# Expert 1's tokens gathered as whole rows and turned on TensorE, in a routed mixture of experts on one core

## The chip, the cores and the metric

The kernel runs on one core of one Trainium2 chip. The metric is the device time of one launch in microseconds (us). The engines are PE (TensorE, with PEld for its weight loads), DVE (VectorE), ACT (ScalarE), POOL (GpSimd) and SP (SyncE); each runs its own instruction stream, and semaphores tie them together.

## The reference

Three stages follow each other. Linear attention over 4 batches, 8 heads, 576 positions gives 2304 rows of 512 numbers. They go through a mixture of experts, and its result through a gated unit:

```
top2 = np.argpartition(-noisy_logits, 2, axis=1)[:, :2]     # of 8 experts
for e in range(E):
    for k in range(2):
        mask = top2[:, k] == e
        h = np.maximum(x[mask] @ w1[e], 0.0)                 # 512 -> 1024
        out[mask] += top2_w[mask, k, None] * (h @ w2[e])     # 1024 -> 512
...
gate = 1.0 / (1.0 + np.exp(-(x @ w_gate)))                   # 512 -> 1536
return (gate * (x @ w_val) @ w_out).astype(np.float32)
```

All of it is in float32.

## The kernel before

Every product of float32 numbers is made of three matmuls of two parts, a high one that ACT makes (a copy into a rounded format) and a low one that DVE makes (the number less its high part): high by high, high by low, low by high. So each weight piece costs one "split" on ACT (L634 for w1, L637 for w2) and one on DVE (L635, L638). The pieces come from memory by SP into four buffers (`raw`), and a buffer is loaded again once DVE's part of its split has read it. A function `pump` adds to a credit with each step of PE's work and hands out the next splits while the credit lasts; its argument is the PE time of the step.

The experts run one after the other. Each takes up to 624 tokens in five blocks of 128 (the last of 112). For expert e:

- `gather` (L691) fetches a block's token rows by POOL's indirect DMA. Expert 0, and blocks 0 and 1 of expert 1, are fetched as whole rows of 528 numbers by the list `lsb`; the other blocks as four quarters of 132 by the list `lsq`, which is made from `lsb` by four small matmuls (`psq`) and a DVE instruction (L1509).
- `scale` multiplies the rows by a factor that they carry, into `xs` (L710) or in place (L723), on an engine that the caller names.
- `expert_in` (L737) turns the block: whole rows by four PE transposes into a PSUM tile `pxT` (L746), quarters by one DVE instruction into `xT` (L750). ACT then writes the high part `xh` (L753) and DVE the low part `xl` (L754).
- `h_step`, for expert 0 `h_first`, multiplies by w1 into `ph` (L763); ACT makes `hh` (L768) and DVE `hl` (L769) of the result.
- `y_step` multiplies one block by w2 into `py` (24 matmuls, L807); ACT copies to `yo` (L812) and sends that to memory (L814).

Expert 0 goes in two parts: blocks 0 and 1 early, blocks 2 to 4 later. The change lies in the stretch between, from the gathering of blocks 2 to 4 of expert 0 to the first matmul of expert 1. There the loop runs over f = 0 to 7: `h_first` for pair f // 2 at even f, a `pump` at every f, expert 1's gathers and scales; then, for blocks 2, 3 and 4 of expert 0, expert 1's `expert_in` of the blocks that are due and one `y_step`. The w2 products of expert 0 for block b are called y_step(0, b) here.

POOL and SP run in the order in which the program is written, DVE from this stretch on, and ACT within the loop; PE's order, and ACT's beside the loop, is set by a list scheduler. PSUM holds two `ph` tiles and four smaller ones, which `pxT`, `py`, `psq` and `pcnt` share: a new one waits until the readers of the one that it replaces are done. In the trace's names numbers are left out: `w_0h` is the high part of piece 0 of some weight.

Of the kernel before, what the change touches and what calls it, by code (L numbers as in the profile page):

```python
# [9 lines left out]
FT = mybir.dt.float32  # L10
FR = mybir.dt.float32r
BF = mybir.dt.bfloat16
HF = mybir.dt.float16
# [4 lines left out]
OP = mybir.AluOpType  # L18
# [21 lines left out]
HL_COST = 0.85  # L40
# [32 lines left out]
def tile_linear_attention_moe_glu(  # L73
# [16 lines left out]
    nc = tc.nc  # L90
    B, H, S, D = q.shape
    N, E = noise.shape
    DM = H * D
# [8 lines left out]
    NB = CAP_BLOCKS  # L102
# [21 lines left out]
    sml = ctx.enter_context(tc.tile_pool(name="sml", bufs=2))  # L124
# [17 lines left out]
    def take(shape, dt, name):  # L142

        i = free.popleft()
        return i, wp.tile(shape, dt, tag="w", name=name)

    def wt(shape, dt, name):

        i, t = take(shape, dt, name)
        free.append(i)  # L150
        return t
# [7 lines left out]
    def et(shape, dt, name):  # L159
        return ep.tile(shape, dt, tag="e", name=name)  # L160
# [9 lines left out]
    def pa(shape, name):  # L170
        return psA.tile(shape, FT, tag="a", name=name)
# [18 lines left out]
    def in_order(names):  # L190
        return tc.manual_schedule(engines={getattr(mybir.EngineType, x) for x in names.split()})

    ctx.enter_context(in_order("SP Pool"))
    first = ctx.enter_context(ExitStack())
# [16 lines left out]
    for i in range(B // 2):  # L211
        x = wt([128, 2, H, D], FT, f"vrem{i}")
# [35 lines left out]
    x, y = KD * 2 * E, KD * 2 * E + NT * E  # L248
# [37 lines left out]
    sel = cst.tile([128, 4, 128], HF, name="sel")  # L286
# [12 lines left out]
    TOK = NA - 128  # L299
# [23 lines left out]
    lsq = cst.tile([128, 4, NB * E], I32, name="lsq")  # L323
    quarter = cst.tile([128, 1], FT, name="quarter")
# [251 lines left out]
    raws, wst, places, whole = deque(), {}, {}, set()  # L576
# [83 lines left out]
    def put_back(u):  # L660
        for i in places.pop(u):
            drop((free, i))

    def pump(work_of_pe, own=0.0):

        pos["now"] += work_of_pe
        pos["credit"] = min(pos["credit"] + RATE * work_of_pe - own, CREDIT)
        while tasks and pos["credit"] > 0 and (not raws or raws[0][1] <= pos["now"]):
            x = tasks[0]
            c = SUM_COST if x[0] == "ws" else SPLIT_COST if len(x) < 5 else DOUBLE_COST[x[4]]  # L670
            if not work():
                break
            pos["credit"] -= c
# [6 lines left out]
    XG, XA, XL, HH, HL = {}, {}, {}, {}, {}  # L680

    def behind(x):

        seen = sml.tile([128, 1], FT, name="seen")
        nc.gpsimd.tensor_copy(seen, x)  # L685

    def whole_rows(e, blk):

        return e == 0 or e == 1 and blk < 2

    def gather(e, blk, quarters=(0, 4)):  # L691
        if whole_rows(e, blk):
            x = et([128, XW], FT, "xg")
            a = e == 0 and blk < AB
            ix = lsa[:, blk:blk + 1] if a else lsb[:, blk * E + e:blk * E + e + 1]
            rows_of(x, xbuf[0:NA, :] if a else xbuf, ix)
        else:
            x = XG[e, blk] if quarters[0] else et([128, 4, QW], FT, "xg")
            for b in range(*quarters):
                rows_of(x[:, b], xbuf.rearrange("n (a w) -> (n a) w", a=4), lsq[:, b, blk * E + e:blk * E + e + 1])  # L700
        XG[e, blk] = x

    def rows_of(x, src, ix):
        nc.gpsimd.indirect_dma_start(out=x, out_offset=None, in_=src,  # L704
                                     in_offset=bass.IndirectOffsetOnAxis(ap=ix, axis=0))

    def scaled_rows(x, eng, xs):

        v = x.rearrange("p (a w) -> p a w", a=4)
        eng.tensor_mul(xs.rearrange("p (c a j) -> p a c j", a=4, j=32),  # L710
                       v[:, :, 0:128].rearrange("p a (c j) -> p a c j", j=32),
                       v[:, :, 128:, None].to_broadcast([128, 4, KD, 32]))
        return xs

    def scale(e, blk, eng):
        x = XG[e, blk]
        if whole_rows(e, blk):
            i, t = take([128, DM], FT, f"xs{e}_{blk}")
            XG[e, blk] = scaled_rows(x, eng, t)
            places["xs", e, blk] = i,  # L720
        else:
            xv = x[:, :, 0:128].rearrange("p b (c j) -> p b c j", j=32)
            eng.tensor_mul(xv, xv, x[:, :, 128:, None].to_broadcast([128, 4, KD, 32]))  # L723
# [761 lines left out]
    with tc.high_priority():  # L1485
        pl = pa([128, NB * E], "plist")
        for g in range(len(groups)):
            add_list(pl, slice(0, NB * E), g, g == 0, g == len(groups) - 1)
        nc.vector.tensor_scalar(lsb, pl, float(TOK), None, op0=OP.add)
        for blk in range(AB, NB):  # L1490
            gather(0, blk)
    for blk in range(AB, NB):
        scale(0, blk, nc.vector)
    pos["hold"] = False
    for blk in range(AB, NB):
        expert_in(0, blk)

# [1 line left out]
        load_piece(nc.scalar)  # L1499
    raws = deque((x, 0.0) for x, _ in raws)  # L1500
    pos["dma"] = 0.0


    lsf = sml.tile([128, NB * E], HF, name="lsf")
    nc.vector.tensor_copy(lsf, pl)
    psq = pa([128, 4, NB * E], "psq")
    for b in range(4):
        nc.tensor.matmul(psq[:, b], sel[:, b], lsf, start=True, stop=True)
    nc.vector.tensor_scalar(lsq, psq, quarter, 4.0 * TOK, op0=OP.add, op1=OP.add)  # L1509

    pc = pa([128, E], "pcnt")
    nc.tensor.matmul(pc, ones, before[:, len(groups)], start=True, stop=False)
# [10 lines left out]
    for e in range(1, E):  # L1523
        nc.vector.tensor_add(base[:, e:e + 1], base[:, e - 1:e], cf[:, e - 1:e])
    nc.vector.tensor_copy(cnt[:, E:2 * E], base)

    first.close()
    ctx.enter_context(in_order("DVE"))
    for e in range(E):
        last = e == E - 1  # L1530
        if e == 1:
            banks.close()
            psP = moe.enter_context(tc.tile_pool(name="psH", bufs=3, space=bass.MemoryType.PSUM, reuse_waits="tile"))
            psA = moe.enter_context(tc.tile_pool(name="psY", bufs=2, space=bass.MemoryType.PSUM, reuse_waits="tile"))
        order = ExitStack()
        if e == 0:
            order.enter_context(in_order("Activation"))
        for f in range(FC):
            if e:
                h_step(e, f)  # L1540
            elif f % 2 == 0:
                h_first(f // 2, 1)
            if f % 2:
                put_back(("w1", e, f // 2))
            pump(*(3.53, HL_COST) if e else (4.15, 0.5))
            if e or f > 1:
                fill()
            i = f
            if e == 0:

                for blk in range(NB - 1) if f == 0 else ():
                    gather(1, blk)
                if f == 1:
                    for blk in range(2):
                        scale(1, blk, nc.gpsimd)
                    gather(1, NB - 1)
                if f > 1 and f % 2:
                    scale(1, f // 2 + 1, nc.gpsimd)
            elif not last:
                if f:  # L1560
                    behind(HH[e, (f - 1) // 2].bitcast(FT)[:, (f - 1) % 2, 0:1])
                gather(e + 1, i // 2, (2 * (i % 2), 2 * (i % 2) + 2))
                if i % 2 and i > 1:
                    scale(e + 1, i // 2 - 1, nc.gpsimd)
        order.close()
        nxt = 0
        for blk in range(AB if e == 0 else 0, NB) if not last else ():
            was = nxt
            while nxt < (NB if blk >= NB - 2 else blk + 1):
                if nxt == 2 and e:  # L1570
                    scale(e + 1, NB - 1, nc.gpsimd)
                if nxt == 0 and e:
                    scale(e + 1, NB - 2, nc.gpsimd)
                with tc.high_priority(1):
                    expert_in(e + 1, nxt)
                if nxt == 0 and e:
                    gather(e + 1, NB - 1)
                nxt += 1
            if (e, blk) == (2, 0):
                tc.mark_branch_hint_location("overflow", engines=ENGINES)  # L1580
            with in_order("PE Activation") if (e, blk) == (1, 2) else nullcontext():
                y_step(e, blk, lambda f: ask_overflow() if (e, blk, f) == (1, 2, 3) else None)

            if (e, blk) != (2, NB - 1):
                pump(5.45, IN_COST * (nxt - was))
                if e:
                    fill()
        if not last:
            for i in range(FP):
                put_back(("w2", e, i))  # L1590
        if e == 2:
            assert len(filled) > OVB
            overflow()
            pump(5.45, IN_COST * (nxt - was))
# [31 lines left out]
    for c in range(NCH):  # L1626
        for p in range(FP2):
            for n in PRODUCTS:
                x = (c, p, n) if n != 1 else (c + (p + 1) // FP2, (p + 1) % FP2, n)
# [163 lines left out]
```

## Time and profile before

| what | value |
|---|---|
| median of 3 runs | 940.29 us (938.28 to 942.1) |
| profiled execution | 948.44 us, its span 946.3 us |
| PE busy | 914.1 us, 97% of the span |
| DVE, ACT, POOL busy | 73%, 46%, 40% |

The span runs from the first to the last instruction that the profiler saw; 2.1 us lie outside of it. Busy time is the time in which an engine had an instruction under way. Times within the execution are counted from the span's start.

### The profile page before, as it was taken

The page shows a single profiled execution, that of the slowest core. Times are in us where ns is not written, and L with a number is a line of the kernel's source. Part 1 is how long each engine was busy: PE and PEld are TensorE (multiplying, and loading weights), DVE is VectorE, ACT ScalarE, POOL GpSimd, SP SyncE. Part 2 cuts the span into 40 slices and gives each one's busy share as a digit, 9 for nine tenths or more (in the row PEclk, how much of TensorE's full clock was granted, in tenths as well). Part 3 has the DMA queues.
Part 4 walks back from the last instruction along what each step waited for, and adds up shares of the span by engine and source line. Part 5 has one row for each costly group of instructions (what it writes and reads, how often), then busy time and mean ns, then how long its engine had stood idle before and what let it go on. Part 6 is the DMA issues. An engine that isn't in the chain of part 4 may idle for free.

```text
span 946.3 us, 14307 instructions
## 1 busy us (share of the span) xinstructions
PE 914.1 (97%) x5153; PEld 791.4 (84%) x5155; DVE 689.5 (73%) x1033; ACT 439.5 (46%) x659; POOL 382.4 (40%) x370
## 2 busy tenths in 40 slices
PE   7987989999999999999999998999999999999998
PEld 4876779989798998989899897888888888888886
DVE  1588687787879787788856567987977776866463
ACT  1674354343433343424333675655545554554451
POOL 2141472737466482855600373342355636300000
PEclk9997999999999999999999999999999999999999
DMA  9985578777867566666744475798477777986784
GB/s 262 286 267 177 172 213 294 253 255 257 269 210 229 183 219 194 206 212 209 238 133 144 133 231 166 246 302 275 145 252 266 254 227 270 345 279 200 216 254 98
DMA packets 134378, 213.91 MB, mean 226 GB/s; under 512 B 20384, under 2 KB 65952, under 8 KB 134304
## 3 DMA queue, kind: packets, MB, share of 16 engines
q1 hardware_dynamic: 116496, 179.82, 59.0%
q0 software_dynamic: 7664, 20.26, 7.6%
q10 hardware_dynamic: 10144, 12.88, 4.0%
q8 instruction: 41, 0.67, 0.3%
q14 instruction: 33, 0.27, 0.1%
HBM read 140.94 MB, written 71.97 MB: 225 GB/s over the span
## 4 chain that ended last, share of the span: by engine, by line
PE 66%; DVE 3%; ACT 1%; issue 1%; DMA 0%; another core or an unknown queue 0%; DVEq 0%; ACTq 0%
PE py L807 14%; PE ph L763 14%; PE pga L1164 12%; PE poa L1343 7%; PE pgc L1164 6%; PE poc L1343 3%; PE pgb L1164 3%; PE pout L1313 2%; PE pob L1343 2%; PE pgv L1132 2%; DVE wt L984 1%; DVE xf L1062 0%; PE px L1030 0%; ACT yg L952 0%; ACT w L983 0%
## 5 line engine op out<-in xcount | busy, mean ns | idle before, releaser
L704 POOL DMA_INDIRECT xg<-xbuf,lsq x132 | 154.2, 1168 | 48.5 <-issue 30.5
L984 DVE TENSOR_TENSOR wt<-lw,wt 128x512 fp32r<-128x512 f32 x84 | 69.5, 833 | 34.1 <-ACT wt L983 30.9
L768 ACT ACTIVATE hh<-ph 128x624 fp32r<-128x624 f32 (+1 forms) x60 | 41.7, 696 | 99.7 <-PE ph L763 86.9
L769 DVE SCALAR_TENSOR_TENSOR hl<-ph,hh 128x624 fp32r<-128x624 f32 (+1 forms) x60 | 48.8, 813 | 48.0 <-ACT hh L768 36.3
L704 POOL DMA_INDIRECT yg<-ybuf,slot x36 | 40.2, 1117 | 83.1 <-issue 60.6
L723 POOL TENSOR_TENSOR xg<-xg 128x512 f32<-128x512 f32 x33 | 36.5, 1108 | 40.3 <-DMA xg<-xbuf,lsq 39.9
L753 ACT ACTIVATE xh<-xT 128x512 fp32r<-128x512 f32 (+3 forms) x40 | 21.1, 544 | 63.7 <-DVE xT L750 58.3
L983 ACT ACTIVATE wt<-lw 128x512 fp32r<-128x512 f32 x84 | 49.8, 621 | 0.0
L1201 POOL TENSOR_TENSOR qt<-qv 128x512 f32<-128x512 f32 x12 | 20.5, 1711 | 65.8 <-DVE qv L1188 32.3
L1178 ACT ACTIVATE q<-pga 128x1024 f32<-128x1024 f32 x24 | 24.7, 1028 | 45.2 <-PE pga L1164 43.9
L754 DVE TENSOR_TENSOR xl<-xT,xh 128x512 fp32r<-128x512 f32 (+3 forms) x40 | 24.3, 618 | 26.6 <-ACT xh L753 25.9
L685 POOL COPY seen<-hh 128x1 f32<-128x1 f32 x42 | 17.1, 407 | 65.2 <-ACT hh L768 64.7
L763 PE MATMUL ph<-xl,w_0h 128*128 128x312 f32 (+2 forms) x128 | 40.5, 316 | 2.4 <-DVE xl L754 2.4
L763 PE MATMUL ph<-xh,w_3h 128*128 128x312 f32 (+2 forms) x128 | 39.2, 306 | 2.5 <-DVE hl L769 2.5
L763 PE MATMUL ph<-xh,w_0h 128*128 128x312 f32 (+2 forms) x128 | 40.4, 316 | 1.0 <-ACT xh L753 1.0
L763 PE MATMUL ph<-xh,w_0l 128*128 128x312 f32 (+2 forms) x128 | 40.3, 315 | 0.3 <-PEq L842 0.3
L812 ACT ACTIVATE yo<-py 128x512 f32<-128x512 f32 (+1 forms) x40 | 23.5, 589 | 36.3 <-PE py L807 30.6
L763 PE MATMUL ph<-xh,w_3l 128*128 128x312 f32 (+2 forms) x128 | 39.3, 307 | 0.0
L763 PE MATMUL ph<-xh,w_1h 128*128 128x312 f32 (+2 forms) x128 | 39.3, 307 | 0.0
L763 PE MATMUL ph<-xh,w_2l 128*128 128x312 f32 (+2 forms) x128 | 39.2, 306 | 0.0
L763 PE MATMUL ph<-xl,w_1h 128*128 128x312 f32 (+2 forms) x128 | 39.2, 306 | 0.0
L763 PE MATMUL ph<-xh,w_1l 128*128 128x312 f32 (+2 forms) x128 | 39.1, 306 | 0.0
(559 smaller groups left out, 3125.2 us busy)
## 6 DMA issues: line engine op xcount, KB each, us to landing
raw<-in_moe_w_dram SPq DMA_DIRECT2D x60, 512.0 KB
lw<-wbuf SPq DMA_DIRECT2D x84, 256.0 KB
gr<-qbuf SPq DMA_DIRECT2D x42, 512.0 KB
ybuf<-yo ACTq DMA_DIRECT2D x32, 256.0 KB
ybuf<-zero SPq DMA_DIRECT2D x29, 256.0 KB
raw<-in_moe_w_out_dram SPq DMA_DIRECT2D x12, 512.0 KB
raw<-in_moe_w_gate_dram SPq DMA_DIRECT2D x12, 512.0 KB
raw<-in_moe_w_val_dram SPq DMA_DIRECT2D x12, 512.0 KB
```

What stands on the lines that cost most here:

```text
L704: nc.gpsimd.indirect_dma_start(out=x, out_offset=None, in_=src, in_offset=bass.IndirectOffsetOnAxis(ap=ix, axis=0))
L723: eng.tensor_mul(xv, xv, x[:, :, 128:, None].to_broadcast([128, 4, KD, 32]))
L754: nc.vector.tensor_sub(XL[e, s][:, :, a:z], pt[:, :, o:o + z - a], XA[e, s][:, :, a:z].bitcast(FT))
L763: nc.tensor.matmul(ph, w[:, c, j], x[e, s][:, c, :], start=(n == 0), stop=(n == 3 * KD - 1))
L768: nc.scalar.activation(hh, ph, AF.Relu)
L769: nc.vector.scalar_tensor_tensor(hl, ph, 0.0, hh.bitcast(FT), op0=OP.max, op1=OP.subtract)
L807: nc.tensor.matmul(py[0:m], x[:, f % 2, t], w[:, f % 2, :], start=(n == 0), stop=(n == 3 * FC - 1))
L983: nc.scalar.activation(hi, src, AF.Copy)
L984: nc.vector.tensor_sub(lo, src, hi.bitcast(FT))
L1164: nc.tensor.matmul(ps[:, j, 0:HT[c]], w[:, a, k, s], x[:, k, :], start=(first and i == 0), stop=(i == 5), skip_group_check=not first)
L1178: nc.scalar.activation(q[name], src, AF.Copy)
L1343: nc.tensor.matmul(ps[:, j, 0:HT[c]], w, g[x][1][:, f, :], start=(first and u + f + i == 0), stop=(u == FP3 - 1 and f + i == 3), skip_grou ...
```

## The change

Blocks 2 to 4 of expert 1 are gathered as whole rows too, five indirect DMAs in place of two and twelve. They are scaled into tiles of the pool that holds the gathered rows, and turned on PE. All five scales of expert 1 go from POOL to DVE. The gathers of blocks 0 and 1 and their scales stand before the loop, those of blocks 2 to 4 at f = 0 to 2, and their scales at f = 3, 5 and 7. The list `lsq` and its matmuls are made behind the counts, and its input `lsf` right behind `lsb`. The written order of DVE and ACT begins three `expert_in` earlier. `pump` is told 2.1 in place of 4.15 at f = 1 and 3, so fewer splits are handed out there. Lines behind L716 move down by three.

```diff
@@ -686,7 +686,7 @@
 
     def whole_rows(e, blk):
 
-        return e == 0 or e == 1 and blk < 2
+        return e < 2
 
     def gather(e, blk, quarters=(0, 4)):
         if whole_rows(e, blk):
@@ -714,7 +714,10 @@
 
     def scale(e, blk, eng):
         x = XG[e, blk]
-        if whole_rows(e, blk):
+        if e and blk > 1 and whole_rows(e, blk):
+            XG[e, blk] = scaled_rows(x, eng, et([128, DM], FT, "xs"))
+            places["xs", e, blk] = ()
+        elif whole_rows(e, blk):
             i, t = take([128, DM], FT, f"xs{e}_{blk}")
             XG[e, blk] = scaled_rows(x, eng, t)
             places["xs", e, blk] = i,
@@ -1487,11 +1490,17 @@
         for g in range(len(groups)):
             add_list(pl, slice(0, NB * E), g, g == 0, g == len(groups) - 1)
         nc.vector.tensor_scalar(lsb, pl, float(TOK), None, op0=OP.add)
+        lsf = sml.tile([128, NB * E], HF, name="lsf")
+        nc.vector.tensor_copy(lsf, pl)
         for blk in range(AB, NB):
             gather(0, blk)
     for blk in range(AB, NB):
         scale(0, blk, nc.vector)
     pos["hold"] = False
+    first.close()
+    ctx.enter_context(in_order("DVE"))
+    order = ExitStack()
+    order.enter_context(in_order("Activation"))
     for blk in range(AB, NB):
         expert_in(0, blk)
 
@@ -1499,14 +1508,6 @@
         load_piece(nc.scalar)
     raws = deque((x, 0.0) for x, _ in raws)
     pos["dma"] = 0.0
-
-
-    lsf = sml.tile([128, NB * E], HF, name="lsf")
-    nc.vector.tensor_copy(lsf, pl)
-    psq = pa([128, 4, NB * E], "psq")
-    for b in range(4):
-        nc.tensor.matmul(psq[:, b], sel[:, b], lsf, start=True, stop=True)
-    nc.vector.tensor_scalar(lsq, psq, quarter, 4.0 * TOK, op0=OP.add, op1=OP.add)
 
     pc = pa([128, E], "pcnt")
     nc.tensor.matmul(pc, ones, before[:, len(groups)], start=True, stop=False)
@@ -1523,18 +1524,21 @@
     for e in range(1, E):
         nc.vector.tensor_add(base[:, e:e + 1], base[:, e - 1:e], cf[:, e - 1:e])
     nc.vector.tensor_copy(cnt[:, E:2 * E], base)
-
-    first.close()
-    ctx.enter_context(in_order("DVE"))
+    psq = pa([128, 4, NB * E], "psq")
+    for b in range(4):
+        nc.tensor.matmul(psq[:, b], sel[:, b], lsf, start=True, stop=True)
+    nc.vector.tensor_scalar(lsq, psq, quarter, 4.0 * TOK, op0=OP.add, op1=OP.add)
+    for blk in range(2):
+        gather(1, blk)
+    for blk in range(2):
+        scale(1, blk, nc.vector)
+
     for e in range(E):
         last = e == E - 1
         if e == 1:
             banks.close()
             psP = moe.enter_context(tc.tile_pool(name="psH", bufs=3, space=bass.MemoryType.PSUM, reuse_waits="tile"))
             psA = moe.enter_context(tc.tile_pool(name="psY", bufs=2, space=bass.MemoryType.PSUM, reuse_waits="tile"))
-        order = ExitStack()
-        if e == 0:
-            order.enter_context(in_order("Activation"))
         for f in range(FC):
             if e:
                 h_step(e, f)
@@ -1542,20 +1546,15 @@
                 h_first(f // 2, 1)
             if f % 2:
                 put_back(("w1", e, f // 2))
-            pump(*(3.53, HL_COST) if e else (4.15, 0.5))
+            pump(*(3.53, HL_COST) if e else (2.1 if f in (1, 3) else 4.15, 0.5))
             if e or f > 1:
                 fill()
             i = f
             if e == 0:
-
-                for blk in range(NB - 1) if f == 0 else ():
-                    gather(1, blk)
-                if f == 1:
-                    for blk in range(2):
-                        scale(1, blk, nc.gpsimd)
-                    gather(1, NB - 1)
+                if f + 2 < NB:
+                    gather(1, f + 2)
                 if f > 1 and f % 2:
-                    scale(1, f // 2 + 1, nc.gpsimd)
+                    scale(1, f // 2 + 1, nc.vector)
             elif not last:
                 if f:
                     behind(HH[e, (f - 1) // 2].bitcast(FT)[:, (f - 1) % 2, 0:1])
```

The first place is ACT around the last `hh` of expert 0 (`hh0_3`): `w1_2_0` is the first w1 piece of expert 2, `pxT_1807` and `pxT_1814` are blocks 0 and 1 of expert 1, `py_1827` is y_step(0, 2). Before:

```order
L768 ACTIVATE hh0_3_1764<-ph_1766 128x2x368 [waits PE_49,Pool_49]
L634 ACTIVATE w1_2_0h_1794<-raw_1706,gcol_162 128x1024 [waits DMAHW4_49,Pool_49]
L753 ACTIVATE xh1_0_1803<-pxT_1814 128x4x128 [waits PE_49]
L812 ACTIVATE yo_1852<-py_1827 128x4x4x32 [waits PE_49]
L814 DMA ybuf_94<-yo_1852 128x512 [waits Activation_49]
```

With the change, `pxT_1801`, `1808`, `1815` and `1857` being blocks 0 to 3 of expert 1, and `py_1824` y_step(0, 2):

```order
L771 ACTIVATE hh0_3_1757<-ph_1759 128x2x368 [waits PE_49,Pool_49]
L756 ACTIVATE xh1_0_1797<-pxT_1815 128x4x56 [waits PE_49]
L756 ACTIVATE xh1_0_1797<-pxT_1808 128x4x128
L756 ACTIVATE xh1_0_1797<-pxT_1801 128x4x128 [waits PE_49]
L815 ACTIVATE yo_1849<-py_1824 128x4x4x32 [waits PE_49]
L817 DMA ybuf_94<-yo_1849 128x512 [waits Activation_49]
L634 ACTIVATE w1_2_0h_1787<-raw_1701,gcol_162 128x1024 [waits DMAHW6_49]
L605 ACTIVATE wo_0_0_1852<-raw_1739 128x512 [waits DMAHW1_49,DVE_49]
```

The high part `w1_2_0h` stood right behind `hh0_3`; now it stands behind the `yo` of y_step(0, 2) and its DMA.

The second place is DVE behind the last `hl` of expert 0 (`hl0_3`), with the low part of the same piece, `w1_2_0l`. Before:

```order
L769 SCALAR_TENSOR_TENSOR hl0_3_1765<-ph_1766,hh0_3_1764 128x2x368 [waits Activation_49]
L635 SCALAR_TENSOR_TENSOR w1_2_0l_1795<-raw_1706,gcol_162,w1_2_0h_1794 128x1024 [waits DMAHW4_49,Activation_49]
L754 TENSOR_TENSOR xl1_0_1804<-pxT_1807,xh1_0_1803 128x4x128
L754 TENSOR_TENSOR xl1_0_1804<-pxT_1814,xh1_0_1803 128x4x128 [waits Activation_49]
L750 STREAM_TRANSPOSE xT_1821<-xg_1642 128x4x4x32 [waits DMASW2_49,DMASW1_49,DMASW7_49,DMASW0_49,Pool_49]
```

With the change, `xs_1755` and `xs_1794` being the scaled rows of blocks 3 and 4 of expert 1:

```order
L710 TENSOR_TENSOR xs_1755<-xg_1654 128x4x4x32 [waits DMASW0_49,DVE_49]
L772 SCALAR_TENSOR_TENSOR hl0_3_1758<-ph_1759,hh0_3_1757 128x2x368 [waits Activation_49]
L635 SCALAR_TENSOR_TENSOR w1_2_0l_1788<-raw_1701,gcol_162,w1_2_0h_1787 128x1024 [waits DMAHW6_49,Activation_49]
L710 TENSOR_TENSOR xs_1794<-xg_1695 128x4x4x32 [waits DMASW1_49,PE_49]
L757 TENSOR_TENSOR xl1_0_1798<-pxT_1801,xh1_0_1797 128x4x128 [waits PE_49]
L757 TENSOR_TENSOR xl1_0_1798<-pxT_1808,xh1_0_1797 128x4x128
L757 TENSOR_TENSOR xl1_0_1798<-pxT_1815,xh1_0_1797 128x4x56
```

The scale of block 4, `xs_1794`, and the low parts `xl` of all blocks stand behind `w1_2_0l`, which needs `w1_2_0h` from ACT.

The third place is PE from the end of y_step(0, 2) to the start of y_step(0, 3). Before, `py_1868` is y_step(0, 3):

```order
L807 MATMUL py_1827<-w2_0_3h_1442,hh0_3_1764 128x512 [waits Activation_49]
L807 MATMUL py_1827<-w2_0_3l_1443,hh0_3_1764 128x512
L807 MATMUL py_1827<-w2_0_3h_1442,hl0_3_1765 128x512 [waits DVE_49]
L807 MATMUL py_1827<-w2_0_3h_1442,hh0_3_1764 128x512
L807 MATMUL py_1827<-w2_0_3l_1443,hh0_3_1764 128x512
L807 MATMUL py_1827<-w2_0_3h_1442,hl0_3_1765 128x512
L807 MATMUL py_1868<-w2_0_0h_1370,hh0_0_1597 128x512
```

With the change, `py_1871` is y_step(0, 3):

```order
L810 MATMUL py_1824<-w2_0_3h_1442,hl0_3_1758 128x512 [waits DVE_49]
L810 MATMUL py_1824<-w2_0_3h_1442,hh0_3_1757 128x512
L810 MATMUL py_1824<-w2_0_3l_1443,hh0_3_1757 128x512
L810 MATMUL py_1824<-w2_0_3h_1442,hl0_3_1758 128x512
L749 MATMUL pxT_1857<-ident_215,xs_1755 128x128 [waits Activation_49]
L749 MATMUL pxT_1857<-ident_215,xs_1755 128x128 x3
L749 MATMUL pxT_1864<-ident_215,xs_1794 128x128 [waits DVE_49]
L749 MATMUL pxT_1864<-ident_215,xs_1794 128x128 x2
L810 MATMUL py_1871<-w2_0_0h_1370,hh0_0_1605 128x512 [waits DVE_49]
```

Where y_step(0, 3) followed y_step(0, 2) without a wait, seven transposes of blocks 3 and 4 stand between them now, and three waits: on ACT for the first transpose of block 3, on DVE for the first of block 4, on DVE for `py_1871`.

## Rows read from the trace of the kernel before

**Rows 1.** The page: span, busy time of each engine, chain that ended last

```profile
span 946.3 us, 14307 instructions
...
PE 914.1 (97%) x5153; PEld 791.4 (84%) x5155; DVE 689.5 (73%) x1033; ACT 439.5 (46%) x659; POOL 382.4 (40%) x370
...
PE 66%; DVE 3%; ACT 1%; issue 1%; DMA 0%; another core or an unknown queue 0%; DVEq 0%; ACTq 0%
```

**Rows 2.** Timeline of PE: start, us, what, [idle time before and its releaser]

```profile
110.27 1.55 PE L746 MATMUL pxT<-ident,xs 128*128 128x128 f32 x12
...
112.39 0.17 PE L1512 MATMUL pcnt<-before,ones 128*128 128x8 bf16 x1 [0.47 <-DVE lsq L1509]
...
113.08 0.44 PE L763 MATMUL ph<-xh,w_0h 128*128 128x368 f32 x1 [0.50 <-ACT xh L753]
...
114.12 0.44 PE L763 MATMUL ph<-xl,w_0h 128*128 128x368 f32 x1 [0.43 <-DVE xl L754]
...
130.06 0.44 PE L763 MATMUL ph<-xh,w_3h 128*128 128x368 f32 x1 [2.55 <-DVE hl L769]
...
138.31 0.50 PE L807 MATMUL py<-w_3h,hh 128*128 128x512 f32 x1 [0.43 <-ACT hh L768]
...
139.74 0.50 PE L807 MATMUL py<-w_3h,hl 128*128 128x512 f32 x1 [0.70 <-DVE hl L769]
...
140.77 0.39 PE L807 MATMUL py<-w_0h,hh 128*128 128x512 f32 x1
...
151.72 0.30 PE L763 MATMUL ph<-xh,w_0h 128*128 128x312 f32 x1
```

**Rows 3.** Timeline of DVE, same columns

```profile
107.77 0.69 DVE L710 TENSOR_TENSOR xs<-xg 128x512 f32<-128x512 f32 x1 [1.28 <-DMA xg<-xbuf,lsb]
...
121.64 3.86 DVE L635 SCALAR_TENSOR_TENSOR w_0l<-raw,gcol,w_0h 128x1024 fp32r<-128x1024 f32 x1
125.42 1.27 DVE L635 SCALAR_TENSOR_TENSOR w_1l<-raw,gcol,w_1h 128x1024 fp32r<-128x1024 f32 x1
...
137.62 1.24 DVE L638 TENSOR_TENSOR w_3l<-raw,w_3h 128x1024 fp32r<-128x1024 f32 x1 [0.75 <-ACT w_3h L637]
138.78 0.91 DVE L769 SCALAR_TENSOR_TENSOR hl<-ph,hh 128x736 fp32r<-128x736 f32 x1
...
140.81 1.27 DVE L754 TENSOR_TENSOR xl<-pxT,xh 128x512 fp32r<-128x512 f32 x2
```

**Rows 4.** Timeline of ACT (ACTq issues its DMAs), same columns

```profile
129.08 1.06 ACT L637 ACTIVATE w_0h<-raw 128x1024 fp32r<-128x1024 f32 x1 [3.68 <-DMA raw<-in_moe_w_dram]
...
136.52 1.06 ACT L637 ACTIVATE w_3h<-raw 128x1024 fp32r<-128x1024 f32 x1 [1.39 <-DMA raw<-in_moe_w_dram]
...
138.15 1.14 ACT L634 ACTIVATE w_0h<-raw,gcol 128x1024 fp32r<-128x1024 f32 x1
...
140.97 0.60 ACT L812 ACTIVATE yo<-py 128x512 f32<-128x512 f32 x1 [1.19 <-PE py L807]
141.60 0.36 ACTq L814 DMA_DIRECT2D ybuf<-yo  x1
```

**Rows 5.** Timeline of POOL, same columns

```profile
122.33 2.07 POOL L710 TENSOR_TENSOR xs<-xg 128x512 f32<-128x512 f32 x2
```

**Rows 6.** Stretches: length, busy time of PE, PEld, DVE, ACT, POOL, PE's granted clock

```profile
18.60:21.30 2.70, 0.01 (x1) 0.04 (x1) 0.00 (x0) 0.76 (x2) 0.00 (x0) 0.73 1.13 271
21.30:26.60 5.30, 5.30 (x56) 4.85 (x58) 0.69 (x1) 1.25 (x3) 0.00 (x0) 0.50 1.13 317
...
74.00:77.60 3.60, 0.00 (x0) 0.00 (x0) 3.59 (x11) 1.04 (x3) 0.00 (x0) 1.00 0.72 204
78.00:88.00 10.00, 7.56 (x39) 7.08 (x38) 7.42 (x28) 1.19 (x2) 4.32 (x5) 0.50 0.48 180
...
127.50:130.00 2.50, 0.02 (x1) 0.00 (x0) 2.50 (x3) 0.92 (x1) 1.89 (x3) 1.00 1.03 365
130.00:134.00 4.00, 3.94 (x23) 3.94 (x24) 3.85 (x3) 2.36 (x4) 2.67 (x4) 1.00 0.88 308
```

## The prediction

> **What bounds the kernel now.** The page comes first [rows 1]: PE is busy for 914.1 of 946.3 us, and the chain that ended last lies on PE, so time is won or lost only where PE waits. The diff works between the gathers of expert 0's late blocks and the first matmul of expert 1, so the timeline of PE there comes next [rows 2]: from 110.27, when PE turns blocks 2 to 4 of expert 0, to 151.72, when expert 1 begins, 41.45 us. PE idles there six times: 0.47, 0.50 and 0.43 at the front (1.40 together), 2.55 before the last `ph` of expert 0, and 0.43 and 0.70 before the last matmuls of y_step(0, 2), 1.13 together. That is 5.1 us, and the change can win no more than this. The timelines of DVE, ACT and POOL then say why. The wait of 2.55 is for `hl`, and DVE is held up by `w_0l`, which took 3.86 where the next split of the same kind took 1.27 [rows 3]; POOL's two multiplications of 2.07 run beside it [rows 5]. The 1.13 hang on the raw weights: ACT's last w2 split starts at 136.52, when its raw lands [rows 4], and `w_3l` and `hl` follow it on DVE [rows 3].
>
> **The front.** `lsq` and its wait for `psq` stood ahead of the low parts on DVE and go behind the counts. The last low part still needs the last `xh` of ACT, so I take 0.5 off the 1.40; the ends are 0 and 1.4.
>
> **The wait for hl.** POOL no longer multiplies, so `w_0l` should take 1.27. From 121.64, three splits and `hl` make 121.64 + 3 x 1.27 + 0.91 = 126.4, the fourth split now standing behind this `hl`. PE, which waited from 127.51 (130.06 - 2.55), reaches this `ph` earlier now, at about 126.3, because three matmuls of y_step(0, 2) move behind it. So 2.55 goes, or 2.0 if the split stays longer than 1.27.
>
> **Twelve transposes more.** Twelve took 1.55 at 110.27 [rows 2]; this is added whole, as PE is what counts: 0.65 for the five that lie beside y_step(0, 2) and y_step(0, 3), and 0.9 for the seven between them. The three DVE transposes that they replace were not waited for by PE and win nothing there. The five scales cost DVE 5 x 0.69 [rows 3]; two stand before the loop, where DVE has room, one ahead of the third `hl`, one ahead of the last, one further on, and these last two are in the sums below.
>
> **The end of y_step(0, 2).** It hangs on the last `hl`, and that on the raws. Before, DVE had freed the first raw buffer at 125.50 (121.64 + 3.86), and the last of the four raws came 11.0 later. With `w_0l` at 1.27 the buffer is free at 122.9, so the last raw comes at 133.9 by the same pace, at about 133.0 if it gains from quarter gathers that no longer run beside it. I take 133.0, with 132.5 and 133.9 as ends. Behind it follow 1.06 on ACT [rows 4], 1.24 on DVE, the scale of block 3 with 0.69, `hl` with 0.91 [rows 3]: 136.9. Before, y_step(0, 2) ended 1.08 after this `hl` (140.77 - 138.78 - 0.91), so it ends at 138.0 now, between 137.5 and 138.9. PE by itself could have been there at 140.77 - 0.5 - 2.55 - 1.13 + 0.5 (four of the transposes) = 137.1, so 0.9 of the 1.13 remains.
>
> **A new wait.** The order rows show it. DVE's `w1_2_0l`, a split for expert 2 that nobody needs soon, waits for `w1_2_0h`, which on ACT now stands behind the `yo` of y_step(0, 2). Behind `w1_2_0l` on DVE wait the scale of block 4 and every `xl` of expert 1, and these keep PSUM tiles, which the transposes of block 4 and y_step(0, 3) need. On PE everything stands behind them. Before, ACT had done this split at 138.15, ahead of the `yo` [rows 4], and y_step(0, 3) needed nothing new. From the end of y_step(0, 2): `yo` starts 0.20 later (140.97 - 140.77) and takes 0.60, its DMA is issued by 140.97 + 0.99 = 141.96 (so 1.2 in all) [rows 4]; `w1_2_0h` takes 1.14, `w1_2_0l` 1.27, the scale 0.69, two low parts 1.27 [rows 3]. That is 5.6, and 5.5 with the small overlap of rows in one queue. In it PE does seven transposes, 0.9, so 4.6 is idle, 3.5 of it in one piece before block 4. The ends are 4.9 (y_step(0, 3) needs but one low part) and 6.0 (it needs three).
>
> **Sum without the clock.** y_step(0, 3) starts at 138.0 + 5.5 = 143.5. From there to expert 1 it is 151.72 - 140.77 = 10.95 and one transpose more: 154.6, so 2.9 later. By terms: -0.5 - 2.55 - 0.2 + 0.65 + 5.5 = 2.9. The ends are about 1.5 and 4.3. PE's 97% leave little behind this point that could swallow a delay, and the instructions of expert 1 onward stand as before.
>
> **The clock.** PE's clock is at its full level, 2.4 GHz, beside these waits. Three idle times tell what another can do [rows 6]. After 2.5 us without work at 127.5 the clock stayed at 1.00. After 3.6 us at 74.0 it was 0.50 (1.2 GHz) for the ten us from 78, of which PE was busy for 7.56; after 2.7 us from 18.6 it was 0.50 for 5.3 us of unbroken work. The new gap, 3.5 us in one piece within 5.5 with 0.9 of work, is nearer to the two after which it fell. At half the clock, half the busy time is lost: 2.65 by the short case, 3.8 by the long, 0 if it stays. I take 2.3, since part of the slow time may lie in the gap itself, as 2.4 of the ten us at 78 were idle. The Trainium skill ("TensorE: Matmul & The Clock Gate", section "HAM oscillation — how this bites in real kernels") says that waits for data between bursts of matmuls put the array back to half its clock and that the next burst begins there. By that rule the term is paid in full, up to 2.65; by the gap at 127.5 alone it would be nothing; the rows at 21.3 and 78 agree with the rule.
>
> **Forecast.** 2.9 + 2.3 = 5.2 us more. The profiled execution would take 948.44 + 5.2 = 953.6; that execution lies 8 us above the median of the runs, and the difference carries over: 940.29 + 5.2 = 945.5. Its own range is 943.5 to 947.5. What a measurement can tell from no change is about 0.5%, 4.7 us here, so this forecast lies just beyond it.
>
> **Rivals.** First, the gap comes and the clock stays at 1.00, as after the idle time at 127.5: 940.29 + 2.9 = 943.2, no difference that can be told. For it: work lies in the gap. Against it: 3.5 us is longer than the 2.7 after which it fell.
>
> Second, not slower: the gap is covered, because `w1_2_0l` doesn't come last. It decides whether the scale of block 4 is ready when y_step(0, 2) ends. Then only the first two transposes' wait for `yo` (0.9) remains, and the sum is -0.5 - 2.55 - 0.2 + 1.55 + 0.9 = -0.8, and -2.6 if the raws come so early that the rest of the 1.13 and the 0.9 go too: 938.6, or 939.5 in the middle. Were all six idle times gone and only the transposes paid, it would be -3.6, 936.7. For it: DVE and POOL have less to do. Against it: DVE and ACT keep the written order.
>
> Third, slower still: the raw of `w1_2_0` lands late. SP issues it behind stores of zeros, and raws came some 2.5 apart ((136.52 - 129.08) / 3 [rows 4]). It decides once the raw comes later than 1.2 after the end of y_step(0, 2), 139.2; one raw's time later the gap grows by 2 and the clock costs 2.65: 940.29 + 2.9 + 2 + 2.65 = 947.8.
>
> **How the numbers follow.** The forecast has 0.55, the clock that stays 0.20, the covered gap 0.17, the late raw 0.08. Slower by over 0.5%: 0.6 of the forecast's 0.55, the late raw's 0.08, 0.02 of the clock that stays, 0.43 in all. Faster by over 0.5% needs less than 935.6 and more than the idle times of this stretch give, so only an error of mine or of the measurement: 0.06. The rest, 0.51, is within 0.5%. The range reaches from 939.0, into the covered gap, to 948.0, over the late raw.
>
> **What would show it.** In the profile of the changed kernel: `w_0l` of 1.3 us at about 121.6, and no idle time over 0.5 before the last `ph` of expert 0; y_step(0, 2) ending near 138; then a gap on PE with `w1_2_0l` on DVE waiting for ACT, y_step(0, 3) some 5.5 later, a granted clock of 0.50 for some microseconds behind it, and expert 1 at 155 to 157 rather than 151.72. The prediction is wrong if DVE's scale of block 4 is done before y_step(0, 2) ends, if the clock stays at 1.00, or if expert 1 begins before 152.

## The result, and the profile after

| | median | range, runs |
|---|---|---|
| before, beside the changed kernel | 941.19 us | 938.28 to 943.92, 6 |
| changed | 950.03 us | 948.69 to 953.53, 6 |
| ratio | 1.0088 | 95%: 1.0065 to 1.011 |

That is 8.8 us more where 5.2 were forecast, and above the range's end of 948.0. On two more chips the same kernel gave 1.009 [1.006, 1.0119] and 1.0062 [1.0044, 1.008], which is 7.1 and 5.9 us by the medians. The profiled execution took 950.87 us. Its page, against [rows 1]:

```profile
span 948.7 us, 14317 instructions
...
PE 916.2 (97%) x5167; PEld 792.4 (84%) x5167; DVE 684.4 (72%) x1035; ACT 438.0 (46%) x659; POOL 363.7 (38%) x356
```

The shares say nothing of the change; the timeline of PE does. It answers to [rows 2], with the same columns (start, us, what, idle time before and its releaser):

```profile
109.10 1.48 PE L749 MATMUL pxT<-ident,xs 128*128 128x128 f32 x12
...
111.16 0.26 PE L1529 MATMUL psq<-lsf,sel 128*128 128x40 f16 x4 [0.56 <-DVE xl L757]
...
112.29 0.44 PE L766 MATMUL ph<-xl,w_0h 128*128 128x368 f32 x1 [0.25 <-DVE xl L757]
...
134.42 0.50 PE L810 MATMUL py<-w_3h,hl 128*128 128x512 f32 x1 [0.28 <-DVE hl L772]
...
136.30 0.66 PE L749 MATMUL pxT<-ident,xs 128*128 128x128 f32 x4 [0.69 <-ACT yo L815]
...
140.41 0.90 PE L749 MATMUL pxT<-ident,xs 128*128 128x128 f32 x3 [3.46 <-DVE xl L757]
141.01 0.79 PE L810 MATMUL py<-w_0h,hh 128*128 128x512 f32 x1
...
153.45 0.30 PE L766 MATMUL ph<-xh,w_0h 128*128 128x312 f32 x1
```

The wait of 2.55 for `hl` is gone. Behind y_step(0, 2) stand 0.69 for the `yo` and 3.46 under the name of `xl`. Expert 1 starts 44.35 us after the first twelve transposes, 41.45 before. DVE, against [rows 3], and ACT, against [rows 4], show why:

```profile
119.27 1.28 DVE L635 SCALAR_TENSOR_TENSOR w_0l<-raw,gcol,w_0h 128x1024 fp32r<-128x1024 f32 x1 [1.10 <-ACT w_0h L634]
...
133.45 0.92 DVE L772 SCALAR_TENSOR_TENSOR hl<-ph,hh 128x736 fp32r<-128x736 f32 x1
137.87 1.29 DVE L635 SCALAR_TENSOR_TENSOR w_0l<-raw,gcol,w_0h 128x1024 fp32r<-128x1024 f32 x1 [3.50 <-ACT w_0h L634]
139.07 0.68 DVE L710 TENSOR_TENSOR xs<-xg 128x512 f32<-128x512 f32 x1
139.68 1.58 DVE L757 TENSOR_TENSOR xl<-pxT,xh 128x512 fp32r<-128x512 f32 x3
```

```profile
130.61 1.06 ACT L637 ACTIVATE w_3h<-raw 128x1024 fp32r<-128x1024 f32 x1 [1.53 <-DMA raw<-in_moe_w_dram]
...
135.65 0.60 ACT L815 ACTIVATE yo<-py 128x512 f32<-128x512 f32 x1 [2.09 <-PE py L810]
136.28 0.36 ACTq L817 DMA_DIRECT2D ybuf<-yo  x1
136.69 1.15 ACT L634 ACTIVATE w_0h<-raw,gcol 128x1024 fp32r<-128x1024 f32 x1 [0.44 <-ACT yo L815]
```

The `w_0h` at 136.69 is w1_2_0h. DVE has nothing to do for 3.50 until it is there, then splits, scales block 4 and makes the low parts; PE's seven transposes and y_step(0, 3) come behind. The clock in stretches of PE (columns as in [rows 6]):

```profile
139.00:140.20 1.20, 0.00 (x0) 0.00 (x0) 1.20 (x3) 0.00 (x0) 0.00 (x0) 1.00 1.07 409
140.20:143.60 3.40, 3.19 (x10) 2.50 (x11) 2.85 (x7) 2.10 (x4) 0.00 (x0) 0.51 0.43 138
143.60:150.00 6.40, 6.40 (x29) 5.12 (x28) 6.16 (x12) 1.06 (x2) 0.00 (x0) 0.99 0.67 205
```

At the end of the gap the clock falls to half its level for 3.4 us, as after the two long gaps of [rows 6].

For the comparison with other runs two lengths are read from ACT's timeline: "the stretch", from the last `ha` of expert 0 to the first `hh` of expert 1, and "expert 2", from its first `hh` to the second of expert 3. "Expert 1" runs from its first `hh` to that of expert 2. Five profiled executions stand on each side: the kernel before three times, with fewer splits alone and with three more buffers alone (both below); the changed kernel four times and with one more buffer. Their means:

| | before | changed | difference |
|---|---|---|---|
| from the start to the first `ha` | 87.3 | 87.3 | 0.0 |
| the stretch | 58.06 | 61.68 | +3.6 |
| expert 1 | 54.81 | 54.95 | +0.1 |
| expert 2 | 60.89 | 62.87 | +2.0 |
| the span | 945.6 | 951.6 | +6.0 |

The profile of [rows 2] is not like the other four on its side. In those four PE's clock falls in the stretch as well, at the front, behind the short waits around the first `ph`, and the wait for `hl` before the last `ph` is then 0.94 to 0.97 us, or none (with fewer splits alone), in place of 2.55. The stretch is hardly longer for it, 57.80 to 58.45 against 57.91. First a repeat of the kernel before, with the clock at the front (columns as in [rows 6]) and that wait, then the execution of [rows 2] at the same place:

```profile
109.00:111.50 2.50, 1.09 (x11) 0.61 (x8) 2.18 (x5) 1.41 (x3) 1.26 (x2) 1.00 0.67 219
111.80:115.00 3.20, 3.20 (x12) 3.20 (x11) 1.78 (x12) 0.00 (x0) 2.29 (x4) 0.50 1.02 345
```

```profile
127.35 0.44 PE L763 MATMUL ph<-xh,w_3h 128*128 128x368 f32 x1 [0.94 <-DVE hl L769]
```

```profile
111.50:114.50 3.00, 1.59 (x13) 1.10 (x12) 2.52 (x9) 1.52 (x3) 1.59 (x2) 1.00 0.75 240
114.50:118.00 3.50, 3.50 (x23) 3.50 (x22) 1.76 (x11) 0.00 (x0) 2.58 (x4) 1.00 0.98 333
```

With half of PE's busy time at half clock counted as lost, an estimate, such a fall costs 1.6 to 1.7 us. The changed kernel has none at the front and one behind the gap, in the one with one more buffer two in a row (3.0 lost). In the stretch the means lose 1.3 us to the clock before and 1.9 after. Expert 2 has a fall too, behind the wait for the last `yo`, in one of the five before and in two of the five changed ones, here in one of these:

```profile
264.70:267.90 3.20, 3.20 (x9) 2.32 (x8) 2.32 (x6) 2.01 (x3) 0.00 (x0) 0.50 0.73 248
```

So 0.3 of the 2.0 in expert 2 is the clock.

### The profile page after: what moved, and what is told of

Read it like the earlier page. It is cut to its first block, busy times and chain, and to the rows that moved or that the text cites. A ratio compares the mean times of both kernels' runs of the same rounds, so it can differ in the third digit from the quotient of the medians.

```text
span 948.7 us, 14317 instructions
## 1 busy us (share of the span) xinstructions
PE 916.2 (97%) x5167; PEld 792.4 (84%) x5167; DVE 684.4 (72%) x1035; ACT 438.0 (46%) x659; POOL 363.7 (38%) x356
## 4 chain that ended last, share of the span: by engine, by line
PE 59%; DVE 4%; DMA 3%; ACT 2%; issue 2%; POOL 1%; SPq 0%; DVEq 0%; ACTq 0%
PE py L810 12%; PE ph L766 12%; PE pga L1167 12%; PE poa L1346 7%; PE pgc L1167 6%; PE poc L1346 3%; PE pgb L1167 3%; PE pout L1316 2%; PE pob L1346 2%; PE pgv L1135 2%; DMA yg<-ybuf,slot 1%; DMA raw<-in_moe_w_val_dram 1%; DMA wbuf<-ws4a 1%; POOL yg L704 1%; DMA raw<-in_moe_w_dram 0%
## 5 line engine op out<-in xcount | busy, mean ns | idle before, releaser
L704 POOL DMA_INDIRECT xg<-xbuf,lsq x120 | 137.6, 1146 | 58.0 <-issue 27.5
L756 ACT ACTIVATE xh<-xT 128x512 fp32r<-128x512 f32 (+3 forms) x36 | 19.2, 548 | 65.6 <-DVE xT L753 64.8
L726 POOL TENSOR_TENSOR xg<-xg 128x512 f32<-128x512 f32 x30 | 33.3, 1110 | 35.9 <-DMA xg<-xbuf,lsq 29.0
L766 PE MATMUL ph<-xh,w_2h 128*128 128x312 f32 (+2 forms) x128 | 39.2, 307 | 0.4 <-DVE hl L772 0.4
```

The source lines that it names most:

```text
L766: nc.tensor.matmul(ph, w[:, c, j], x[e, s][:, c, :], start=(n == 0), stop=(n == 3 * KD - 1))
```

## The experiments

First the two kernels once more, on another chip: the kernel before against itself gave 0.9999 [0.9974, 1.0024], the changed one 1.009. On a third chip one further execution of each took 951.92 and 960.44 us. In all executions of the changed kernel the two idle times stood again, 0.69 and 3.45 to 3.46.

**The split that comes too early in the order.** In the changed kernel, nothing is handed out at f = 7:

```diff
-            pump(*(3.53, HL_COST) if e else (2.1 if f in (1, 3) else 4.15, 0.5))
+            if e or f < FC - 1:
+                pump(*(3.53, HL_COST) if e else (2.1 if f in (1, 3) else 4.15, 0.5))
```

> The changed kernel, but at f = 7 of expert 0 no split is handed out, so that the first w1 piece of expert 2 goes behind the low parts of expert 1's blocks on DVE and behind the yo on ACT. Theory gap: the wait of 3.5 us before the transposes of block 4 falls to under 1.5, the clock stays at 1.00, and the kernel takes 4 to 5 us less than the changed one (about 945, 1.004 of before). Rival, the loss lies behind this stretch: the stretch gets as short, and the time stays at 949 to 950.

Measured: 1.0008 [0.998, 1.0036], 948.11 us on the chip where the changed kernel had 955.22 and the one before 948.08. The stretch is 55.71, shorter than before; expert 2 stays long, 64.29. It contains one fall of the clock, 1.7; the stretch contains none. DVE now goes from `hl` to the low parts without a stop, and so does PE:

```profile
132.81 0.92 DVE L772 SCALAR_TENSOR_TENSOR hl<-ph,hh 128x736 fp32r<-128x736 f32 x1
133.64 0.68 DVE L710 TENSOR_TENSOR xs<-xg 128x512 f32<-128x512 f32 x1
134.24 1.58 DVE L757 TENSOR_TENSOR xl<-pxT,xh 128x512 fp32r<-128x512 f32 x3
...
138.95 1.28 DVE L635 SCALAR_TENSOR_TENSOR w_0l<-raw,gcol,w_0h 128x1024 fp32r<-128x1024 f32 x1 [2.20 <-ACT w_0h L634]
```

```profile
134.00:146.00 12.00, 11.83 (x55) 9.05 (x55) 9.12 (x17) 5.96 (x9) 1.04 (x2) 1.00 0.86 281
```

The same split still waits 2.20, but behind the scale and three low parts, and PE is busy for 11.83 of 12.00 us at full clock. Without this one split in its place the change costs nothing.

**The clock alone.** The transposes of block 3 are done eight times over, so that PE has work in the gap; the waits stay:

```diff
-            for c in range(KD):
+            for c in range(KD * (8 if (e, blk) == (1, 3) else 1)):
+                c = c % KD
```

> The changed kernel with the four transposes of block 3 of expert 1 done eight times over (28 more, the same result written again), in the wait for the scale of block 4. The wait on DVE stays, PE works through it. Theory clock: the half clock behind the gap goes, y_step(0, 3) starts when it did, and the time falls by 1.5 to 3.5 us against the changed kernel. Rival, the wait alone: the dip costs nothing that can be told, and the time stays within 1 us of the changed kernel (1.009 of before).

Measured: 1.0056 [1.0023, 1.0088]; the stretch is 59.78. The stretch behind the gap at full clock:

```profile
136.00:140.00 4.00, 3.71 (x32) 3.48 (x32) 2.34 (x3) 1.93 (x4) 0.00 (x0) 1.00 1.03 381
140.00:150.00 10.00, 9.79 (x44) 7.81 (x45) 8.96 (x18) 3.48 (x6) 0.00 (x0) 1.00 0.53 157
```

With nothing else changed, work that computes nothing new made the stretch 1.9 us shorter than the mean of 61.68 (1.2 shorter than the shortest, 60.93). So the clock's part is near 1.6, which is half of the 3.19 busy at 140.20: with what the clock cost each of them taken off, the five of the changed kernel come to 59.8 on the mean, next to the 59.78 here.

**ACT's order kept.** Here ACT keeps the written order through the y_steps, which puts w1_2_0h ahead of the `yo`:

```diff
-        order.close()
+        if e:
+            order.close()
...
+        order.close()
```

> The changed kernel with the written order of ACT kept on through expert 0's y_steps, so that the high part of the split w1_2_0 goes ahead of the xh and the yo; splits, gathers, scales and PE transposes as in the changed kernel. Theory order: what costs is that this one ACT instruction stands behind the yo. w1_2_0l no longer waits for the yo, the idle time between y_step(0, 2) and y_step(0, 3) falls from 4.7 us to under 1, the stretch to expert 1 is 2 us shorter than in the kernel before, and the time is 0.996 to 1.001 of before. Rival, the twelve transposes and the PSUM tiles that wait for DVE cost by themselves: a wait of 2 us or more remains and the time is 1.004 to 1.008.

Measured: 1.0066 [1.0038, 1.0094], the stretch 59.69. ACT and PE:

```profile
135.88 1.15 ACT L634 ACTIVATE w_0h<-raw,gcol 128x1024 fp32r<-128x1024 f32 x1 [1.55 <-DMA raw<-in_moe_w_dram]
136.94 1.31 ACT L756 ACTIVATE xh<-pxT 128x512 fp32r<-128x512 f32 x3
```

```profile
139.61 1.93 PE L749 MATMUL pxT<-ident,xs 128*128 128x128 f32 x8 [1.99 <-DVE xl L757]
```

The split no longer waits for the `yo`, and starts when its raw lands, ahead of the end of y_step(0, 2). On DVE the split, the scale and the low parts still come one after the other, and PE waits 1.99 for them, the time that the rival gave; 3.4 us at half clock follow, although 1.99 is shorter than the 2.5 of [rows 6] that left the clock at 1.00. Putting the split first on ACT isn't enough, as long as it stands ahead of the scale on DVE.

**The parts of the change.** Fewer splits alone, in the kernel before (`pump` with 2.1 at f = 1 and 3):

> The kernel before with the fewer splits alone (2.1 told at f = 1 and 3), quarters and DVE transposes as before. The split w1_2_0 on ACT still goes ahead of the yo here, but two low parts and the DVE transposes stand behind it. Theory gap: y_step(0, 3) needs no tile that the low parts keep, so no wait over 1 us appears between y_step(0, 2) and y_step(0, 3), and the time is 0.996 to 1.002 of before. Rival, fewer splits cost by themselves, because the raws come later to the rest of the kernel: 1.004 to 1.009.

0.9993 [0.9961, 1.0025], the stretch 58.12, with a fall of the clock at the front as in the repeats of the kernel before: no effect by itself. The changed kernel without this part (4.15):

> The changed kernel with 4.15 told to the handing out of splits at f = 1 and 3, as before. The order of ACT then has the high part of the first w1 piece of expert 2 ahead of the yo again. Theory gap: w1_2_0l no longer waits, the idle time between y_step(0, 2) and y_step(0, 3) falls from 4.7 to 1 to 2 us, 3 to 4.5 us less than the changed kernel (945.5 to 947). Rival, the fewer splits are what saves time before the gap: the wait for hl before the last ph of expert 0 returns with 1 to 2.5 us and the time stays near 949.

1.0028 [1.0004, 1.0052], the stretch 58.62. The wait that the change had removed is back, 1.87 before the last `ph`, with 3.4 us at half clock behind it, and the gap behind y_step(0, 2) is down to 0.47:

```profile
PE ph L766 <- DVE hl L772: 1.9, 1, 1.9
PE pxT L749 <- ACT yo L815: 0.5, 1, 0.5
```

Whole rows alone, in the kernel before (scales on POOL, list and order as there; with the tiles for the scaled rows as in the change):

```diff
-        return e == 0 or e == 1 and blk < 2
+        return e < 2
```

> The kernel before with only the whole rows of blocks 2 to 4 of expert 1 and their PE transposes; scales on POOL, the list and the splits as before. Theory rows: the transposes between y_step(0, 2) and y_step(0, 3) cost a wait of 1 to 2.5 us on PE, since their PSUM tiles come free one by one after the yo and the low parts; 1.002 to 1.006 of before, of which the wait for hl before the last ph of expert 0 keeps its 1 to 2.5 us. Rival, only the split behind the yo costs: no wait over 0.7 there, 0.998 to 1.001.

1.0024 [0.9999, 1.0048], the stretch 57.65. Ahead of y_step(0, 3) PE waits 0.31, as the rival said; the longest waits are 1.45 and 1.09 at the front, with a fall of the clock behind them. What makes it longer than before is expert 2, 62.97, which neither theory had. The changed kernel with this one line undone, so with quarters for blocks 2 to 4, and all the rest of the change:

> The changed kernel with blocks 2 to 4 of expert 1 gathered as quarters and turned on DVE as before; the list behind the counts, the scales on DVE and the fewer splits stay. Theory order: y_step(0, 3) waits for no tile, so no gap; 0.996 to 1.001 of before. Rival, the scales on DVE or the list are what costs: 1.004 or more without a gap on PE.

0.9975 [0.9956, 0.9994], the stretch 54.59: 3.5 us less than before, 1.3 of it the falls of the clock that it doesn't have, and a version that beats both kernels, if by little. DVE's split waits there as long as in the changed kernel, and PE doesn't mind:

```profile
137.73 1.29 DVE L635 SCALAR_TENSOR_TENSOR w_0l<-raw,gcol,w_0h 128x1024 fp32r<-128x1024 f32 x1 [3.72 <-ACT w_0h L634]
```

```profile
141.01 0.49 PE L810 MATMUL py<-w_0h,hh 128*112 128x512 f32 x1 [0.31 <-DVE xl L757]
```

No transposes of blocks 3 and 4 stand on PE ahead of y_step(0, 3), so y_step(0, 3) doesn't wait. This is the same wait on DVE, harmless in one kernel and 4 us in the other. With 4.15 in that version:

> The kernel of the experiment with quarters, with 4.15 told at f = 1 and 3 as before, so that the list behind the counts and the scales on DVE stay alone. Theory: the gain of that kernel comes from the wait for hl before the last ph of expert 0 and needs the fewer splits, so here 1 to 2 us of that wait return: 0.998 to 1.001. Rival, the front and the scales alone bring it: 0.995 to 0.998.

1.0044 [1.0016, 1.0073], outside both forecasts, the stretch 61.34, with several waits of up to 1.94 and a piece at half clock. So, each against the kernel before on its own chip, fewer splits are worth 0.7% in the version with quarters, cost 0.6% in the changed kernel, and do nothing in the one before.

**Expert 2.** It is longer in the kernels with whole rows: 61.66 to 64.64 in ten profiles, 59.55 to 62.60 in seven of kernels with quarters (without the three runs that move the zero fills, below). The ranges overlap by the falls of the clock; with those taken off they are 61.4 to 63.0 and 59.6 to 61.2. On DVE, POOL and SP its instructions stand in the order of before. The waits of PE in expert 2, in a repeat of the kernel before, then in one of the changed kernel (waited for: us, times, longest):

```profile
PE py L807 <- ACT yo L812: 1.9, 1, 1.9
PE ph L763 <- PEq L842: 0.3, 1, 0.3
```

```profile
PE py L810 <- ACT yo L815: 1.4, 2, 1.0
PE py L810 <- ACT hh L771: 0.7, 1, 0.7
PE ph L766 <- DVE hl L772: 0.5, 1, 0.5
PE ph L766 <- PEq L845: 0.3, 1, 0.3
```

ACT ahead of those waits, in the same two executions (expert 1's first `hh` at 152.62 and 156.48):

```profile
220.35 1.06 ACT L637 ACTIVATE w_0h<-raw 128x1024 fp32r<-128x1024 f32 x1 [1.09 <-DMA raw<-in_moe_w_dram]
221.31 1.26 ACT L768 ACTIVATE hh<-ph 128x624 fp32r<-128x624 f32 x2
...
234.02 0.68 ACT L605 ACTIVATE wo<-raw 128x512 f32<-128x512 f32 x1 [3.26 <-DMA raw<-in_moe_w_out_dram]
```

```profile
226.59 1.06 ACT L637 ACTIVATE w_0h<-raw 128x1024 fp32r<-128x1024 f32 x1 [2.04 <-DMA raw<-in_moe_w_dram]
227.56 1.26 ACT L771 ACTIVATE hh<-ph 128x624 fp32r<-128x624 f32 x2
...
240.41 0.67 ACT L605 ACTIVATE wo<-raw 128x512 f32<-128x512 f32 x1 [3.91 <-DMA raw<-in_moe_w_out_dram]
```

Counted from expert 1's first `hh`, the split at 67.73 starts at 70.11 now and the copy of a `wo` piece at 81.40 at 83.93, each behind its raw, and `hh` of expert 2 stands behind them on ACT. PE waits for those `hh` and the `hl` that follow. The list names only 0.7 us more than before; by the starts of PE's matmuls, 0.14 (312 columns) or 0.23 us (512) apart where nothing holds them up, the breaks for `hh` and `hl` make 2.3, those for the `yo` 2.0 against 2.2, which is the 2.1 by which these two executions differ. So raws that come about 2.5 us later cost PE in expert 2. Why they come later was tried in two ways. First, with four zero fills of 256 KB (f = 4 to 7) taken out of expert 1 and done beside expert 2's w2 products:

```diff
-            if e or f > 1:
+            if (e or f > 1) and (e != 1 or f < 4):
                 fill()
...
+                    if e == 2 and blk < 4:
+                        fill()
```

In the kernel before, in the changed one, in the version with quarters, and the changed one as it is:

> The kernel before, with the zero fills of f = 4 to 7 of expert 1 (four DMAs of 256 KB) issued beside expert 2's w2 products instead. Late-raw theory: the extra time that kernels with whole rows lose inside expert 2 comes from raw weights that land about 1 us late there; before, the raws are in time, so taking 1 MB of traffic away from expert 1 gives at most 1 us, ratio 0.999 to 1.000, expert 2 (60 to 61 us) unchanged or 0.5 to 1 shorter, since only the wait for yo remains. Rival (the loss in expert 2 has nothing to do with the raws): also 1.000.

> The changed kernel with the same four fills moved out of expert 1. Late-raw theory: raws of expert 2 come earlier, expert 2 falls from 61.7 to 62.1 us to about 60.5 (no half clock counted), and the ratio to before falls from 1.009 to about 1.006 (5.5 us more), what is left being the stretch ahead of expert 1. Rival: expert 2 stays at 61.7 to 62.1 and the ratio at 1.009.

> The changed kernel with quarters for blocks 2 to 4 of expert 1, and the four fills moved. Both theories: expert 2 was not longer there, so at most 1 us less than the same kernel without the fills moved: ratio 0.996 to 0.998.

> The changed kernel once more, on the same chip, as the base for the others: ratio 1.008 to 1.010, expert 2 at 61.7 to 62.1 us without half clock.

Measured: 1.0017 [1.0002, 1.0033], 1.0114 [1.0086, 1.0142], 0.9997 [0.9979, 1.0015], 1.0062. Expert 2 took 60.80, 64.02, 63.46 (1.7 of it the clock) and 62.94, and expert 1 itself grew to 56.77 and 56.30 in the second and the third. The changed kernel got slower, not faster: its split at 70.11 came at 72.32. Either the traffic of the fills is not what holds the raws up, or what was moved did as much harm where it went. Second, the buffers: the scaled rows take three tiles more from a pool of four.

```diff
                     scale(1, f // 2 + 1, nc.gpsimd)
+                    nc.gpsimd.memset(et([128, DM], FT, "xs")[:, 0:1], 0.0)
```

> The kernel before, with three more tiles taken from the pool that holds the gathered rows (each written with a memset of one column on POOL), as the change takes three for its scaled rows; the order of ACT, DVE, PE and SP stays. Buffer theory: the gathers for expert 2 then fall on other buffers of the four and land otherwise, and expert 2 takes about 62.5 us in place of 60.3 to 61.2, ratio about 1.002. Rival (the order on ACT in expert 1, or when the raws were handed out): 1.000, expert 2 at 60.3 to 61.2.

> The changed kernel with one more tile from that pool, so that the gathers for expert 2 fall on the same buffers as before (5 tiles before, 9 now, four buffers). Buffer theory: expert 2 falls from 61.7 to 62.9 us to about 60.8, ratio 1.004 to 1.006. Rival: expert 2 stays at 61.7 to 62.9, ratio 1.006 to 1.009.

Measured: 1.0017 [0.9992, 1.0042] with expert 2 at 59.55, and 1.0089 [1.0054, 1.0125] with 63.15. The buffers are not the cause. Left is the order on ACT in expert 1: there the scheduler put w1_2_3h ahead of the third `hh`, where before it stood behind it, in the changed kernel and in all but one of its variants with whole rows:

```text
before                                   changed
ACTIVATE wo<-raw x2                      ACTIVATE wo<-raw x2
ACTIVATE hh<-ph 128x624                  ACTIVATE w1_2_3h<-raw
ACTIVATE w1_2_3h<-raw                    ACTIVATE hh<-ph 128x624
```

The one without it is the kernel with ACT's order kept, and its expert 2 took 61.70, no less than the changed kernel's 61.66. So this order isn't shown to be the cause either. It stays open why the raws are late.

## Why the prediction was wrong

Point by point, in its own terms:

- The front: 0.56 and 0.25 are left of 1.40, 0.6 won where 0.5 was taken.
- The wait for `hl`: `w_0l` took 1.28 (1.27 forecast), and the 2.55 went whole. The two multiplications of [rows 5] take 2.07 together. But 2.55 was that execution's; where the clock falls at the front, under 1 us of it is there to win.
- The end of y_step(0, 2): 135.61 (136.30 - 0.69), 26.5 us after the twelve transposes began, where 27.7 was forecast (110.27 to 138.0) and 27.2 was the early end. The last raw's split began 21.5 after that mark, not 22.7. Taking the old pace of the raws was the wrong size; 0.28 of the 1.13 stayed in that execution, up to 0.82 in others.
- The new wait: y_step(0, 3) began 5.4 after y_step(0, 2) ended, 5.5 forecast; 4.15 were idle, 4.6 forecast, 3.46 of it in one piece where 3.5 was said, with DVE's `w_0l` waiting for ACT as written.
- The clock: half its level for 3.4 us, about 1.6 lost, 2.3 taken. Four of the five executions on the side of before lose 1.6 to 1.7 at the front as well; the one of [rows 2] doesn't, so no term has it. None of the three rivals came: the gap was not covered, the clock did not stay, and the raw of w1_2_0 was there before the `yo`'s end. The Trainium skill's rule ("TensorE: Matmul & The Clock Gate", section "HAM oscillation — how this bites in real kernels"), that waits for data between bursts put the array back to half its clock, holds here at 3.46 us and in one run at 1.99, and not at the 2.55 of [rows 2].

In the second rival, 938.6 and 939.5 stand the wrong way round: -0.8 gives 939.5, and 938.6 is the middle.

The sum for the stretch was +5.2 and came out at +3.6, on the mean of five. Of the 3.6, PE's idle time makes 1.7 (4.6 to 6.3 us; by the forecast's terms 4.6 less 0.5, 2.55 and 0.2, so 1.35), the clock 0.5 (2.3 in the forecast), and the rest, 1.4, is work, where 1.55 was added for the twelve transposes. So the mis-sized term of this part is the clock: its fall behind the gap came, but the kernel before mostly pays for one as well. The forecast of this part was too high by 1.6, and still the kernel was slower than the range allowed.

The step that failed is the sentence "PE's 97% leave little behind this point that could swallow a delay, and the instructions of expert 1 onward stand as before". It looked only for something that takes a delay up. The other sign was left out: the order of the splits against the raws isn't held by PE, and expert 2 lost 2.0 us more, 1.6 without the clock, which no term had. Also the sentence isn't true of ACT, where the scheduler moved a split ahead of an `hh` in expert 1. The two parts make 5.6 of the 6.0 that the spans differ by, near the 5.2 of the forecast only because one error is 1.6 too high and the other 2.0 too low, which is luck. By themselves these 5.6 don't lead out of the range: with 940.29 they make 945.9. The medians differ by 5.9 to 8.8, and of these only the 8.8 leads past 948.0 in the same way (5.9 and 7.1 give 946.2 and 947.4); the 0 to 3 us beyond the spans stay open, since single executions of one kernel differ by several us themselves (942.0 to 949.8 for the spans of the kernels that stand for before).

## What to carry to other kernels

When work moves from one engine to PE's queue, read what the engine that feeds it has queued ahead: the same wait of 3.5 us on DVE cost nothing where PE's next products didn't need DVE, and 4 us and the clock where seven transposes stood before them. A split for later that is handed out one step too early is enough; leaving that one out brought 955.22 us back to 948.11. And ask of each edit ahead of a list scheduler whether the order far behind it stays, on every engine, before calling the rest unchanged.

## What the hardware showed that was not expected

A wait of 1.99 us on PE was followed by 3.4 us at half clock, and so were, in a repeat of the kernel before, waits of 0.47, 0.56 and 0.38 with PE busy for 1.09 of 2.50 us, while one of 2.55 before the last `ph` in [rows 2] was not; the length of the last idle time by itself doesn't decide. And a fall of the clock need not cost time: where it cost 1.7 us at the front, the wait for `hl` was 1.6 shorter, and the stretch stayed near 58. Raw loads that SP issued 40.57 and 40.58 us after expert 1's first `hh` were split at 47.63 in one execution of the kernel before and at 48.38 in one of the changed kernel; why the second came 0.75 us later isn't known.
